# Some 390 unread matmuls behind the last useful one, with the moving operand in permuted pieces or the weights at a step

## The chip, the core and the metric

The kernel runs on one core of one Trainium2 chip. The metric is the device time of one execution in microseconds (us); lower is better. A core has five engines with queues of their own: TensorE (PE, with its weight loads shown apart as PEld), VectorE (DVE), ScalarE (ACT), GpSimd (POOL) and SyncE (SP, which here only issues DMAs). Results of PE land in PSUM, which has eight banks; everything that PE reads lies in SBUF, 128 partitions wide.

## The reference

Two stages follow each other. The first is an attention over 8 batches and 8 heads of width 64: 32 global rows attend to all 544 rows, and 512 local rows attend to the global ones and to a window of 32 to each side. The second is a two-layer MLP over all 4352 rows:

```python
x = np.ascontiguousarray(attn_out.transpose(0, 2, 1, 3)).reshape(B * S, H * D)   # 4352 x 512
h = x @ w_in                                                                     # 512 -> 2048
g = 0.5 * h * (1.0 + erf(h * inv_sqrt2))
return (g @ w_out).astype(np.float32)                                            # 2048 -> 512
```

All inputs and the output are float32.

## The kernel before, in words

**Precision.** Apart from the first stretch, which runs plain fp32 matmuls, every product is taken in a rounded 32-bit type (fp32r): an operand is split into a high part, which is the rounded value, and a low part, which is what is left. A product is then three matmuls: high by high, high by low and low by high.

**The MLP.** The rows are cut into 17 chunks of 256: two for each batch, and a last one with key "g" for all the global rows. For a chunk, `ml_hc` makes `h` for one of the 16 blocks of 128 hidden columns: four contraction steps of three matmuls each, whose weights (the stationary operand) are 128 columns of `wh` or `wl` and whose moving operand is 256 columns of `xh` or `xl` (L711 to L713). After the gelu and the split of its result, `ml_o` adds a block to the two output tiles `acc0` and `acc1`: weights are 128 columns of `gh` or `gl`, the moving operand is the 512 columns of `wh` or `wl` (L746 to L748). `ml_e` copies `acc` to `ob`, `ml_w` sends it out.

**The weights.** `w_4` (L175) lays the high parts of `w_in` and `w_out` into tiles of 1024 columns, two blocks of 512 in one tile (`wh`, 16 tiles of 4 KB in each partition). They stay there to the end.

**The order.** A planner written in the kernel sorts all steps by costs and due times and records them one after the other. It also ties every instruction to the one before it on its engine (`behind`), so that each queue stands in the planner's order. The attention of later batches is woven between the MLP of earlier ones; the last stretch of the program, from about 1000 us on, is the MLP of the chunk "g" alone. The last steps are the second half of its output: twelve matmuls into `acc1`, a copy of it on ACT, and DMAs from SP and ACT.

**PSUM.** The pool `ps_h` has two buffers of one bank each. `h` takes them in turn.

Of the kernel before, what the change touches and what calls it, by code (L numbers as in the profile page):

```python
# [8 lines left out]
F32 = mybir.dt.float32  # L9
# [75 lines left out]
def attn_mlp(ctx, tc, q_l, k_l, v_l, q_g, k_g, v_g, w_in, w_out, out):  # L85
    nc = tc.nc
    B, H, S, D = q_l.shape
# [3 lines left out]
    P = 128  # L91
    NCC = DM // P
    NF = FF // P
# [16 lines left out]
    ps_h = ctx.enter_context(tc.tile_pool(name="ps_h", bufs=2, space=PSUM))  # L110
# [7 lines left out]
    for half in range(2):  # L118
        m = (cp if half else mp).tile([P, WF], BF16, name=f"mask{half}")
# [10 lines left out]
    st = {}  # L130

    def copy(e, out, in_):
        if e == "a":
            nc.scalar.activation(out=out, in_=in_, func=AF.Copy)  # L134
        elif e == "v":
            nc.vector.tensor_copy(out=out, in_=in_)  # L136
        else:
            nc.gpsimd.tensor_copy(out=out, in_=in_)
# [5 lines left out]
    wp = ctx.enter_context(tc.tile_pool(name="wp", bufs=2 * NF + 1))  # L144
    wr = ctx.enter_context(tc.tile_pool(name="wr", bufs=NF))
    wraw, wf, wh, wl_ = {}, {}, {}, {}

    def w_load(e, n):
        f = n // 2
        wraw[n] = raw = wr.tile([P, 1024], I32, name="wraw", tag="wr")  # L150
        if n % 2 == 0:
            (nc.sync if e == "s" else nc.scalar).dma_start(
                out=raw.rearrange("p (c x) -> p c x", c=NCC),
                in_=w_in.bitcast(I32).rearrange("(c p) w -> p c w", p=P)[:, :, f * 256:(f + 1) * 256])
        else:
            (nc.sync if e == "s" else nc.scalar).dma_start(out=raw, in_=w_out.bitcast(I32)[f * P:(f + 1) * P, :])
# [18 lines left out]
    def w_4(e, i, n):  # L175
        if i % 2 == 0:
            wh["t"] = wr.tile([P, 1024], F32R, name="wh", tag="wr")
        wh[n] = wh["t"][:, i % 2 * 512:i % 2 * 512 + 512]
        copy(e, wh[n], wf[n])

# [606 lines left out]
    for i, n in enumerate(wl):  # L787
        due = 0.0
        step(("wl", n), w_load, (n,), WLE, due - 6.0, [("w1", wl[i - NW])] if i >= NW else [], [("wr", n)], issues=0.85, size=0.52, after=("wl", wl[i - 1]) if i else None)
        step(("w1", n), w_1, (n,), "av", due - 4.0, [("wl", n)])  # L790
        step(("w2", n), w_2, (n,), "a", due - 3.5, [("w1", n)])
        step(("w3", n), w_3, (n,), "v", due - 2.5, [("w2", n), ("w3", wl[i - 1]) if i else None], frees=[("wr", n)])
        used = [("mo", (0, 0), n // 2)] if n % 2 else [("hc", (0, 0), n // 2, c) for c in range(NCC)] if n // 2 < HQ or n // 2 == NF - 1 else [("h", (0, 0), n // 2)]
        step(("w4", n), w_4, (i, n), "va", due + 60.0, [("w3", wl[NF + i // 2]), ("wl", wl[-1])] + ([("w4", wl[i - 1])] if i else []), [("wr", ("h", n))] if i % 2 == 0 else [])
        step(("w5", n), w_5, (n,), "pv", due + 61.0, [("w4", n), ("w5", wl[i - 1]) if i else ("w3", wl[-1])] + used)

    for n, u in enumerate(units):
        b, half, p = u
        c = 2 * b + half
# [25 lines left out]
        else:  # L825
            last = [("tq", units[NPE - x]) for x in (3, 4)] if n < NPE + 2 else []
# [5 lines left out]
        w = n < NF32  # L832
# [19 lines left out]
        g = (b, p // 2) if half else None  # L852
# [59 lines left out]
    for n, key in enumerate(keys):  # L912
# [6 lines left out]
        for f in range(NF):  # L919
            hb = [("h", (key, f // 2))] if f % 2 == 0 else []  # L920
            w = [("w3", 2 * f)] if not n else [("w5", 2 * f)] if n == 1 else []
# [39 lines left out]
    while stack:  # L961
        x = stack.pop()
# [9 lines left out]
    for nm, x in nodes.items():  # L972
# [3 lines left out]
        else:  # L976
            c = 2 * nm[1][0] + nm[1][1] if len(nm) > 1 and isinstance(nm[1], tuple) else 99
# [7 lines left out]
    for x in nodes.values():  # L985
        y = x["after"]
# [21 lines left out]
    def starts(x, k):  # L1008
        t = x["at"][k]
        n = {}  # L1010
        for kind, y in x["takes"]:
            n[kind] = n.get(kind, 0) + 1
        for kind, m in n.items():
            h = sorted((freed.get(y, 1e9) for y in taken.get(kind, [])), reverse=True)
            i = bufs.get(kind, 1) - m
            if i < len(h):
                if h[i] == 1e9:
                    return None
                t = max(t, h[i] + LAT0)
        if k == "a" and x["size"]:  # L1020
            t = max(t, dma - 1.5)
        return t
# [4 lines left out]
    while any(ready.values()):  # L1027
        can = []
        for k in ENG:
            for x in ready[k]:  # L1030
                t = starts(x, k)
                if t is None:
                    continue
                t = max(t, busy[k])
                if k == "p" or k == "v" and x["port"]:
                    t = max(t, port)
# [11 lines left out]
        t, due, _, x, k = best  # L1048
# [33 lines left out]
    last, taker, w1s = {}, {}, {}  # L1082
# [5 lines left out]
    for t, i, x in order:  # L1088
        x["fn"](x["on"], *x["args"])
        ins = nc.cur_bb.bb.instructions  # L1090
# [12 lines left out]
            taker[kind] = ins[seen].name, ins[seen].engine  # L1103
        seen = len(ins)


# [1 line left out]
_INS = ['q_l', 'k_l', 'v_l', 'q_g', 'k_g', 'v_g', 'moe_w_in', 'moe_w_out']  # L1108
# [26 lines left out]
```

## Time and profile before

| | |
|---|---|
| time, median of 2 runs | 1045.17 us (1043.53 to 1046.81) |
| the profiled execution | 1045.66 us, of which 1043.8 us is the span from the first to the last instruction |
| granted TensorE clock, mean | 0.998 |
| PE busy | 1006.6 us, 96% of the span, 7000 matmuls |
| DVE, ACT, POOL busy | 66%, 65%, 36% |
| chain that ended last | PE 75%, ACT 7%, SP's queue 6%, DMA 5%, DVE 4% |

A matmul's listed duration holds its way through the array, which overlaps the next one; so the listed 0.28 us of a matmul with 256 columns isn't what it costs in a row of them. What it costs is the distance from one start to the next, and that is read from the timeline. A row of the timeline gives the start in us, the duration in us, the engine, the line, the operation, the tiles out<-in, and the shapes (contraction rows * output rows, then rows x columns of the moving operand).

### The profile page before, as it was taken

To read this page: it belongs to the slowest core of one execution; us is meant where nothing else is said; L and a number is where in the kernel's file an instruction comes from. 1 tells how busy PE (TensorE), PEld (TensorE's weight loads), DVE (VectorE), ACT (ScalarE), POOL (GpSimd) and SP (SyncE) were. 2 spreads that over 40 slices of the span, in tenths; PEclk is the share of its full clock that TensorE was granted. 3 is DMA by queue.
4 is the path that set the end of the run, shared out by engine and by line. 5 is a ranking of instruction groups with operands and counts; after the bars stand their busy time and mean duration, and the time that the engine had idled before them with its cause. 6 is when DMAs were issued, how large, how long until landed. Compare 5 with 4: busy or idle time off the path is not lost.

```text
span 1043.8 us, 21420 instructions
## 1 busy us (share of the span) xinstructions
PE 1006.6 (96%) x7000; PEld 894.8 (86%) x7000; DVE 684.9 (66%) x2089; ACT 677.0 (65%) x1617; POOL 379.7 (36%) x427
## 2 busy tenths in 40 slices
PE   3889999999998999999999999999999999999998
PEld 2666689989888989898999989998999989999997
DVE  2878978667676877777775777677776777572000
ACT  2868887667567866677675766677575766674232
POOL 2111576243332533343442524334343525233121
PEclk9999999999999999999999999999999999999999
DMA  6877232223221233223322232313322332101000
GB/s 165 239 207 260 51 72 54 49 45 77 57 59 36 38 77 66 63 39 60 79 43 55 55 82 53 65 31 61 82 39 57 62 71 58 48 14 56 1 21 21
DMA packets 277983, 72.29 MB, mean 69 GB/s; under 512 B 263152, under 2 KB 271344, under 8 KB 277872
## 3 DMA queue, kind: packets, MB, share of 16 engines
q1 hardware_dynamic: 271792, 68.57, 28.7%
q10 hardware_dynamic: 6080, 2.36, 0.9%
q8 instruction: 55, 0.90, 0.4%
q14 instruction: 56, 0.46, 0.1%
HBM read 61.41 MB, written 9.44 MB: 68 GB/s over the span
## 4 chain that ended last, share of the span: by engine, by line
PE 75%; ACT 7%; SPq 6%; DMA 5%; DVE 4%; issue 2%; POOL 1%; ACTq 0%; DVEq 0%; POOLq 0%
PE h L711 10%; PE acc L746 9%; PE h L712 9%; PE h L713 9%; PE acc L748 9%; PE acc L747 9%; PE o L519 5%; PE s L408 4%; PE acc L738 2%; PE t L482 2%; ACT a_t L281 2%; PE h L707 2%; PE go L652 2%; ACT L281 1%; DMA raws<-in_q_l_dram 1%
## 5 line engine op out<-in xcount | busy, mean ns | idle before, releaser
L141 POOL TENSOR_TENSOR gl<-gf,gh 128x512 fp32r<-128x512 f32 x127 | 167.8, 1321 | 400.4 <-ACT gh L134 280.1
L711 PE MATMUL h<-xh,wh 128*128 128x256 f32 x1024 | 296.6, 290 | 1.4 <-ACT gf L281 1.4
L712 PE MATMUL h<-xl,wh 128*128 128x256 f32 x1024 | 286.1, 279 | 0.0
L713 PE MATMUL h<-xh,wl 128*128 128x256 f32 x1024 | 285.6, 279 | 0.0
L746 PE MATMUL acc<-wh,gh 128*128 128x512 f32 x512 | 204.9, 400 | 0.0
L711 PEld LDWEIGHTS h<-xh,wh 128*128 128x128 f32 x1024 | 192.7, 188 | 10.2 <-ACT gf L281 1.8
L748 PE MATMUL acc<-wl,gh 128*128 128x512 f32 x512 | 200.4, 391 | 0.0
L747 PE MATMUL acc<-wh,gl 128*128 128x512 f32 x512 | 200.2, 391 | 0.0
L712 PEld LDWEIGHTS h<-xl,wh 128*128 128x128 f32 x1024 | 193.0, 188 | 5.7 <-issue 0.7
L713 PEld LDWEIGHTS h<-xh,wl 128*128 128x128 f32 x1024 | 193.9, 189 | 0.0
L281 ACT ACTIVATE gf<-h 128x512 f32<-128x512 f32 x136 | 81.2, 598 | 69.4 <-POOL gl L141 34.9
L281 ACT ACTIVATE a_t<-a_t,sm 128x192 f32<-128x192 f32 (+1 forms) x256 | 116.8, 458 | 1.9 <-DVE sm L433 1.1
L748 PEld LDWEIGHTS acc<-wl,gh 128*128 128x128 f32 x512 | 96.1, 188 | 21.1
L427 DVE CUSTOM_DVE_ANT_0 a_t<-s,mask 128x192 f32<-128x192 f32 (+1 forms) x256 | 80.4, 368 | 44.0 <-PE s L408 43.8
L134 ACT ACTIVATE gh<-gf 128x512 fp32r<-128x512 f32 x95 | 60.0, 632 | 75.7 <-PE acc L748 74.7
L746 PEld LDWEIGHTS acc<-wh,gh 128*128 128x128 f32 x512 | 96.3, 188 | 12.2
L747 PEld LDWEIGHTS acc<-wh,gl 128*128 128x128 f32 x512 | 96.4, 188 | 11.2
L134 ACT ACTIVATE at<-t 128x512 fp32r<-128x512 f32 (+1 forms) x112 | 59.5, 542 | 48.2 <-PE t L483 21.2
L502 DVE TENSOR_TENSOR at<-t,at 128x512 fp32r<-128x512 f32 (+1 forms) x112 | 67.5, 617 | 34.6 <-ACT at L134 33.9
L141 POOL TENSOR_TENSOR vs<-vr,vs 128x512 fp32r<-128x512 f32 x56 | 74.6, 1332 | 41.8 <-DVE vs L136 19.9
L281 ACT ACT_TABLE_LOAD x69 | 88.5, 1283 | 1.2
L550 DVE TENSOR_TENSOR xs<-o,xs 64x256 f32<-64x256 f32 x112 | 46.1, 412 | 49.0 <-ACT xs L545 47.9
(132 smaller groups left out, 1736.1 us busy)
## 6 DMA issues: line engine op xcount, KB each, us to landing
wraw<-in_moe_w_out_dram SPq DMA_DIRECT2D x16, 512.0 KB, 7.8
raws<-in_v_l_dram SPq DMA_DIRECT2D x64, 128.0 KB, 2.5
out_dram<-ob SPq DMA_DIRECT2D x32, 256.0 KB, 2.2
raws<-in_k_l_dram SPq DMA_DIRECT2D x224, 36.0 KB, 1.9
vr<-in_v_l_dram SPq DMA_DIRECT2D x113, 64.0 KB, 2.1
wraw<-in_moe_w_in_dram SPq DMA_DIRECT2D x14, 512.0 KB, 7.6
raws<-in_q_l_dram SPq DMA_DIRECT2D x224, 32.0 KB, 1.8
raws<-in_v_g_dram SPq DMA_DIRECT2D x128, 16.0 KB, 1.9
```

Of the source, the lines that this page charges most:

```text
L134: nc.scalar.activation(out=out, in_=in_, func=AF.Copy)
L141: (nc.vector if e == "v" else nc.gpsimd).tensor_sub(**kw)
L281: nc.scalar.activation(func=func, **kw)
L427: nc.vector.tensor_tensor_reduce(out=a_t[:, j, aoff[half][i]:aoff[half][i] + w], in0=s[:, c:c + w], in1=masks[half][i], scale=1.0, scalar= ...
L502: nc.vector.tensor_sub(out=at[:, 1], in0=st.pop((u, "t", j))[:, :n * P].rearrange("p (n q) -> p n q", q=P), in1=at.bitcast(F32)[:, 0])
L519: nc.tensor.matmul(out=o[:, :, qsl], lhsT=l.rearrange("p s e -> p (s e)"), rhs=r, start=(n == 0), stop=(n == 3), skip_group_check=True)
L711: nc.tensor.matmul(out=h, lhsT=hi, rhs=xh, start=(c == 0 and not (key == (0, 0) and f < HQ and f % 2)), stop=False, skip_group_check=True)
L712: nc.tensor.matmul(out=h, lhsT=hi, rhs=xl, start=False, stop=False, skip_group_check=True)
L713: nc.tensor.matmul(out=h, lhsT=lo, rhs=xh, start=False, stop=(c == NCC - 1), skip_group_check=True)
L746: nc.tensor.matmul(out=acc[t], lhsT=gh[:, f % 2, tsl], rhs=hi, start=(f == 0), stop=False)
L747: nc.tensor.matmul(out=acc[t], lhsT=gl[:, f % 2, tsl], rhs=hi, start=False, stop=False)
L748: nc.tensor.matmul(out=acc[t], lhsT=gh[:, f % 2, tsl], rhs=lo, start=False, stop=(f == NF - 1))
```

## The change

Every `wh` tile is remembered in a list `wr_t`. After the planner's steps have all been recorded, 390 more matmuls are recorded and tied to the end of PE's queue (`after_all`). Each reads high parts of weights, both as its stationary and as its moving operand, and writes into a bank of `ps_h` (tiles named `zaa`, `zab` and so on, in the two buffers by turns). Nothing reads these tiles. Each matmul starts its own sum (`start=True, stop=True`).

- `run(a, n, w, b, st_)` is a sequence of n equal matmuls into one bank: weights are 128 columns of the tile T5 that begin at column a, the moving operand is the first w columns of T1. With b over 1, `perm` puts the moving columns and the output columns into another order: the w columns are b parts, and pieces of 16 columns (64 bytes) are taken from the parts by turns. The output is permuted in the same way, so each product lands where it would have.
- With `st_` the weights are 128 columns at a step of 2, 4 or 8 columns.
- `mo` and `h` have the shape of an output step and a hidden step: two banks with three matmuls of 512 columns each, and one bank with twelve of 256, here with b = 2 and the weights moved by x columns. They are run by turns, eight times.

By columns of the moving operand that makes: 256 columns 270 times (6 plain, 80 with b = 2, 32 with b = 4, 40 with weights at a step of 2, 8 at a step of 4, 8 at a step of 8, 96 in the eight `h`), and 512 columns 120 times (48 with b = 2, 24 with weights at a step of 2, 48 in the eight `mo`). The 246 of the `run` calls are the matmuls "of no use" in the change's title; the 144 of `mo` and `h` are as unread.

```diff
     wraw, wf, wh, wl_ = {}, {}, {}, {}
+    wr_t = []
...
             wh["t"] = wr.tile([P, 1024], F32R, name="wh", tag="wr")
+            wr_t.append(wh["t"])
...
+    def after_all(e0):
+        ins = nc.cur_bb.bb.instructions
+        for y in ins[e0:]:
+            if y.engine in last:
+                behind(y, last[y.engine])
+            last[y.engine] = y.name
...
+    def bank(n):
+        return n, ps_h.tile([P, 512], F32, name="z" + next(code), tag="h")
+
+    def perm(x, b):
+        return x if b == 1 else x.rearrange("p (b a i) -> p a b i", b=b, i=16)
+
+    def mm(t, st_, mv, b=1):
+        nc.tensor.matmul(out=perm(t[:, 0:mv.shape[-1]], b), lhsT=st_, rhs=perm(mv, b), start=True, stop=True, skip_group_check=True)
...
+    T1, T2, T3, T5, T6, T7 = (wr_t[i] for i in (1, 3, 5, 7, 9, 11))
+
+    def run(a, n=8, w=256, b=1, st_=None):
+        _, t = bank(0)
+        for _ in range(n):
+            mm(t, T5[:, a:a + 128] if st_ is None else st_, T1[:, 0:w], b)
+
+    def mo(x, b):
+        t = [bank(0)[1] for _ in range(2)]
+        for i in range(2):
+            for m, g in ((T1, 0), (T1, 256), (T2, 0)):
+                mm(t[i], T5[:, 128 * i + g + x:128 * i + g + x + 128], m[:, 0:512], b)
+
+    def h(x, b):
+        _, t = bank(0)
+        for c in range(4):
+            for m, g in ((T3, T2), (T6, T2), (T3, T7)):
+                mm(t, g[:, c * 128 + x:c * 128 + 128 + x], m[:, 0:256], b)
+
+    run(0, 6)
+    for a in (0, 16, 32, 48, 8, 24, 40, 56):
+        run(a, 10, 256, 2)
+    for a in (0, 16, 32, 48, 8, 24, 40, 56):
+        run(a, 6, 512, 2)
+    for a in (0, 16, 32, 48):
+        run(a, 8, 256, 4)
+    for a in (0, 16, 32, 48):
+        run(0, 10, 256, 1, T5[:, a:a + 256:2])
+    for a in (0, 16, 32, 48):
+        run(0, 6, 512, 1, T5[:, a:a + 256:2])
+    run(0, 8, 256, 1, T5[:, 0:512:4])
+    run(0, 8, 256, 1, T5[:, 0:1024:8])
+    for x in (0, 16, 32, 48):
+        for _ in range(2):
+            mo(x, 2)
+            h(x, 2)
+    after_all(e0)
```

PE's queue before ends with the last output tile and the branch to the end of the program (`acc_13652` is `acc1` of the chunk "g"):

```order
L746 MATMUL acc_13652<-wh,gh 128x512
L747 MATMUL acc_13652<-wh,gl 128x512
L748 MATMUL acc_13652<-wl,gh 128x512
L746 MATMUL acc_13652<-wh,gh 128x512
L747 MATMUL acc_13652<-wh,gl 128x512
L748 MATMUL acc_13652<-wl,gh 128x512
L1130 UNCONDITIONAL_BRANCH
```

Now the same place, two lines further down in the file; a row is one instruction or several equal ones, and the bracket names the semaphore that it waits for (`PE_49` is the one that PE itself raises):

```order
L748 MATMUL acc_13652<-wh,gh 128x512
L749 MATMUL acc_13652<-wh,gl 128x512
L750 MATMUL acc_13652<-wl,gh 128x512
L1124 MATMUL zaa<-wh 128x256 [waits PE_49]
L1124 MATMUL zaa<-wh 128x256 x5
L1124 MATMUL zab<-wh 128x8x2x16 [waits PE_49]
L1124 MATMUL zab<-wh 128x8x2x16 x9
L1124 MATMUL zac<-wh 128x8x2x16 [waits PE_49]
L1124 MATMUL zac<-wh 128x8x2x16 x9
```

The new rows stand behind the last useful matmul, and the first matmul of each of the 55 new tiles waits for an earlier one of PE that used the same bank.

The middle of the new rows, on PE, where the permuted sequences with b = 4 give way to the weights at a step, and these to the eight turns of `mo` and `h`:

```order
L1124 MATMUL zaw<-wh 128x4x4x16 x8
L1124 MATMUL zax<-wh 128x256 x10
L1124 MATMUL zay<-wh 128x256 x10
L1124 MATMUL zaz<-wh 128x256 x10
L1124 MATMUL zba<-wh 128x256 x10
L1124 MATMUL zbb<-wh 128x512 x6
L1124 MATMUL zbc<-wh 128x512 x6
L1124 MATMUL zbd<-wh 128x512 x6
L1124 MATMUL zbe<-wh 128x512 x6
L1124 MATMUL zbf<-wh 128x256 x8
L1124 MATMUL zbg<-wh 128x256 x8
L1124 MATMUL zbh<-wh 128x16x2x16 x3
```

Nothing stands between them but more of PE's own rows; the queues of ACT, DVE, POOL and SP hold the same instructions in the same order as before.

More of the change, by code (lines that the diff above doesn't have):

```diff
@@ L1104, in attn_mlp @@
         seen = len(ins)
+    def after_all(e0):
[4 more added lines that the diff above has]
+            last[y.engine] = y.name
+    code = iter([a + b for a in "abcdefghijkmnpqrstuvwxyz" for b in "abcdefghijkmnpqrstuvwxyz"])
+    def bank(n):
[4 more added lines that the diff above has]
+        nc.tensor.matmul(out=perm(t[:, 0:mv.shape[-1]], b), lhsT=st_, rhs=perm(mv, b), start=True, stop=True, skip_group_check=True)
+    e0 = len(nc.cur_bb.bb.instructions)
+    H = [wh[n] for n in range(2 * NF)]
+    LO = [wl_[n] for n in range(2 * NF)]
+    key = "g"
+    X = [st["xh", key, c] for c in range(NCC)]
+    Y = [st["xl", key, c] for c in range(NCC)]
+    G = st[key, "gh", NF // 2 - 1].rearrange("p a b -> p (a b)")
+    T1, T2, T3, T5, T6, T7 = (wr_t[i] for i in (1, 3, 5, 7, 9, 11))
[31 more added lines that the diff above has]
+    after_all(e0)
 _INS = ['q_l', 'k_l', 'v_l', 'q_g', 'k_g', 'v_g', 'moe_w_in', 'moe_w_out']
```

## The prediction

> **What bounds the kernel now.** I read the page first: the busy line of PE, the granted clock and the chain that ended last.
>
> ```profile
> span 1043.8 us, 21420 instructions
> PE 1006.6 (96%) x7000; PEld 894.8 (86%) x7000; DVE 684.9 (66%) x2089; ACT 677.0 (65%) x1617; POOL 379.7 (36%) x427
> PEclk9999999999999999999999999999999999999999
> PE 75%; ACT 7%; SPq 6%; DMA 5%; DVE 4%; issue 2%; POOL 1%; ACTq 0%; DVEq 0%; POOLq 0%
> ```
>
> PE is busy for 96% of the span, holds 75% of the chain, and its clock is granted in full. The change touches only what comes behind PE's last useful matmul, so the next view is the timeline at the end of the span, and the busy time there in two windows (columns: length, then busy us and count of PE, PEld, DVE, ACT, POOL, then the granted clock, the DMA share and GB/s).
>
> ```profile
> 1039.10 0.39 PE L748 MATMUL acc<-wl,gh 128*128 128x512 f32 x1
> 1039.52 0.60 ACT L134 ACTIVATE ob<-acc 128x512 f32<-128x512 f32 x1 [0.76 <-PE acc L748]
> 1040.15 0.87 ACTq L761 DMA_DIRECT2D out_dram<-ob  x2
> 1038.79 2.73 SPq L761 DMA_DIRECT2D out_dram<-ob  x6
> ...
> 1030.00:1039.30 9.30, 9.30 (x48) 7.78 (x46) 0.69 (x1) 1.83 (x3) 0.67 (x1) 1.00 0.00 0
> 1039.30:1043.80 4.50, 0.19 (x1) 0.00 (x0) 0.00 (x0) 0.60 (x1) 0.00 (x0) 0.89 0.45 117
> ```
>
> PE has no gap up to its last matmul. After it come one copy of 0.60 us, the last output DMAs and the end of the program: 4.5 us in which PE is idle. That is all the cover there is for new work at the end of PE's queue.
>
> **What one more matmul costs.** Both shapes of the new matmuls stand in the last stretch, where PE alone works. I take the distance of starts over one hidden block and one output block; the rows between are left out.
>
> ```profile
> 1011.70 0.28 PE L711 MATMUL h<-xh,wh 128*128 128x256 f32 x1
> ...
> 1013.11 0.39 PE L746 MATMUL acc<-wh,gh 128*128 128x512 f32 x1
> ...
> 1014.47 0.28 PE L711 MATMUL h<-xh,wh 128*128 128x256 f32 x1
> ```
>
> Between the first two rows twelve matmuls of 256 columns start: (1013.11 − 1011.70) / 12 = 0.1175 us each. Between the last two stand six of 512 columns: 1.36 / 6 = 0.2267 us each. Each includes its weight load, which runs under the matmul before it. The new matmuls load weights once each too, so these are their prices if neither the order of pieces nor the step of the weights matters.
>
> The Trainium skill has a price for this: "TensorE: Matmul & The Clock Gate", section Back-to-back issue gap, gives N/2.4 + 2.5 ns for an isolated matmul at the full clock, which would be 109 and 216 ns here and a sum of 55.4 us instead of the one below. The trace is 8 to 11 ns above it per matmul, and the trace decides.
>
> **The change part by part.** The list of tiles costs nothing on the chip. The rest is 390 matmuls in PE's queue:
>
> - 270 of 256 columns: 270 × 0.1175 = 31.7 us
> - 120 of 512 columns: 120 × 0.2267 = 27.2 us
> - together 58.9 us.
>
> They could start at 1039.10 + 0.23 = 1039.33 and would be through at 1098.25; the last one, of 256 columns, ends 0.28 − 0.12 = 0.16 us later, at 1098.41. The copy on ACT and the output DMAs don't depend on them and go on as before, now hidden under PE. Then the end of the program follows. Its length I work out from the rows above: SP's six issues take 2.73 us, so the last one starts at about 1041.07. How long it takes to land is in the list of DMA issues (KB each, median us from issue to landing).
>
> ```profile
> out_dram<-ob SPq DMA_DIRECT2D x6, 64.0 KB, 1.8
> ```
>
> It lands at about 1042.9, and the span ends at 1043.8: 0.9 us for the barrier. So the new span is 1098.41 + 0.9 = 1099.3 us. The profiled execution took 1045.66 us for a span of 1043.8, which leaves 1.86 us outside; that makes 1101.2 us, 55.5 us more than before. The profiled run lies 0.5 us above the median of the runs shown, so I say 1101.
>
> **The waits.** The first matmul of each of the 55 tiles waits on PE's own semaphore. Such a wait stands in the program before too, at the second `h` tile of the chunk "g", behind the output step that ends here:
>
> ```profile
> 996.19 0.39 PE L748 MATMUL acc<-wl,gh 128*128 128x512 f32 x1
> 996.42 0.28 PE L711 MATMUL h<-xh,wh 128*128 128x256 f32 x1
> 996.54 0.28 PE L712 MATMUL h<-xl,wh 128*128 128x256 f32 x1
> ```
>
> The distances are 0.23 and 0.12 us, the same as without a wait. In the new code the matmul waited for is the last one of the bank two tiles earlier, and the tile between is at least three matmuls of 512 columns, 0.68 us, against the 0.39 us that one takes in all. Nobody else stands in PE's queue behind these waits that another engine needs. So 0 us; if that cover were gone, each would cost the rest of one matmul, 0.39 − 0.23 = 0.16 us, or 9 us for 55.
>
> **Permuted pieces.** 208 matmuls of 256 columns (16 pieces, 15 breaks) and 96 of 512 (32 pieces, 31 breaks) read and write in pieces of 16 columns. No row of before has such small pieces. The nearest has one break: `o` (L519) reads two pieces of 128 columns and writes two into PSUM.
>
> ```profile
> 627.82 0.64 PE L519 MATMUL o<-at,vs 128*128 128x256 f32 x4
> 628.29 0.42 PE L565 MATMUL sg<-k,gs 128*128 128x288 f32 x2
> ```
>
> Four of them take 628.29 − 627.82 = 0.47 us, 0.1175 each: the break costs nothing that 0.01 us over four matmuls can show. If each break cost 1 ns, the sum would be 208 × 15 + 96 × 31 ns = 6.1 us. At the other end stands half the pace, for which there are rows of the same sizes: the plain fp32 matmuls of the first chunk.
>
> ```profile
> 111.83 1.73 PE h L707 x8
> 113.56 1.72 PE acc L738 x4
> ```
>
> They start 0.216 and 0.43 us apart. At that pace the permuted ones cost 208 × 0.0985 + 96 × 0.203 = 40 us more. I take zero, since the nearest row shows zero; below zero is possible only by a little: the same `h` matmuls run slightly denser elsewhere.
>
> ```profile
> 599.74 0.28 PE L711 MATMUL h<-xh,wh 128*128 128x256 f32 x1
> ...
> 600.64 0.28 PE L713 MATMUL h<-xh,wl 128*128 128x256 f32 x1
> ```
>
> Eight in 0.90 us, 0.1125 each; for all 270 that is a gain of 1.4 us.
>
> **Weights at a step.** 56 matmuls of 256 columns and 24 of 512 load their 128 columns at a step of 8, 16 or 32 bytes. How much room a load has is seen where four follow each other with little else to do:
>
> ```profile
> 603.45 0.46 PEld L610 LDWEIGHTS gt<-ident,sgr 128*128 128x128 f32 x4
> 603.88 0.14 PEld L611 LDWEIGHTS gtg<-ident,sgr 128*128 128x128 f32 x1
> ```
>
> (603.88 − 603.45) / 4 = 0.1075 us for a load of consecutive columns. So a load has 0.01 us to spare under 256 columns and 0.12 us under 512. For a step, PE shows nothing; ACT does, reading every second 32-bit word (L167) against consecutive ones (L134):
>
> ```profile
> L167 ACT ACTIVATE wraw<-wraw 128x512 f32<-128x512 f32 x32 | 20.6, 669 | 0.0
> L134 ACT ACTIVATE ob<-acc 128x512 f32<-128x512 f32 x34 | 19.0, 597 | 10.7 <-PE acc L748 9.8 <-PE o L519 0.6
> ```
>
> That is 1.12 times, and 0.1075 × 1.12 = 0.120 us would add 0.2 us over the 56. I take that, as zero. The bound: twice the load, 0.215 us, costs 56 × 0.0975 = 5.5 us and stays hidden under 512 columns. If it grows with the step (2, 4, 8 times 0.1075), it is 40 × 0.0975 + 8 × 0.3125 + 8 × 0.7425 = 12.3 us.
>
> **The rivals.**
>
> - *Loads at a step are slow.* For it: only 0.01 us of room. Against it: ACT's row. 5.5 to 12.3 us more: 1107 to 1113.
> - *Pieces are slow.* PE breaks its stream at each piece, in SBUF or PSUM. For it: 16 or 32 pieces are far from the two of `o`. Against it: the break of `o` is free. Up to half the pace: 1141.
> - *The new matmuls aren't there.* Nothing reads the `z` tiles, and what turns the program into chip code may leave them out; the time would be 1045. It decides at the count of PE's matmuls, 7000 or 7390. For it: they have no reader. Against it: they stand in the program's order with waits that are kept. Any mixture that stays within 2% (20.9 us) would need the 390 to cost under 20.9 + 4.5 us, 65 ns each, and no row of 128 by 128 weights with 256 columns is under 112.
>
> The Trainium skill speaks for the first two: "SBUF — State Buffer", section SBUF: two separate sides, says that SBUF has lines of 16 bytes that want two hits each, PSUM lines of 8 bytes, and that any non-contiguous PSUM access slows matmuls significantly. Taken at its word that is the second rival; taken by its mechanism, pieces of 64 bytes fill their lines and cost nothing, while weights at a step of 4 or 8 columns hit each line once and pay. The row of `o` agrees with the mechanism more than with the word, though with one break only.
>
> **How the numbers follow.** Forecast, everything at the pace of the rows, with up to 1 ns per break: 72%, 1097 to 1107, likeliest 1101. Slow loads 14%; slow pieces 12%, mostly 1118 to 1141; not there 2%. The lower end takes twice the denser pace (2.7 us) and half the spread of the runs shown (1.6 us) off 1101; the upper end takes in the forecast and the slow loads, and a little of slow pieces: 1118. Outside remain most of slow pieces and the last rival. A measurement of this kernel tells about 2% from no change. Faster 1%, within 2% 2%, slower 97%.
>
> **What would show it.** PE has 7390 matmuls; DVE, ACT and POOL have their counts. The new rows start at 1039.3 without a gap and their starts are 0.117 and 0.227 us apart in every group; the end follows the last by about 1 us. If a group of weights at a step shows more, the first rival holds for it; if the groups with 8x2x16 columns do, the second. A gap at each new tile would show the waits wrong.

## The result and the profile after

The changed kernel takes 1099.99 us (median of 2 runs, 1099.91 to 1100.06) against 1045.17 us (median of 2 runs, 1043.53 to 1046.81). The ratio is 1.0524 with a 95% interval of 1.0453 to 1.0595: slower, by 54.8 us. The profiled execution took 1099.91 us for a span of 1098.1 us, so 1.8 us lie outside it, as before.

The page of the changed kernel, for the same lines as before:

```profile
PE 1069.9 (97%) x7390; PEld 952.6 (87%) x7390; DVE 681.8 (62%) x2089; ACT 676.9 (62%) x1617; POOL 380.2 (35%) x427
PE 82%; ACT 4%; SPq 3%; DVE 3%; DMA 2%; issue 1%; POOL 1%; DVEq 0%; ACTq 0%; POOLq 0%
```

PE has 390 matmuls more, and as many weight loads; DVE, ACT and POOL have the counts of before, and their busy times are within 3.1 us of before. The chain of waits ends in PE now, with the last new tile `zcg`, where before it went over to the copy `ob` on ACT.

The timeline of PE at the end of the changed kernel shows the last useful row and the first new ones, and after that the first tile of each group (start, time to the end of the row's last matmul, then the form and the count). The distance from one tile's start to the next, over the count, is the pace.

```profile
1034.09 0.39 PE L750 MATMUL acc<-wl,gh 128*128 128x512 f32 x1
1034.32 0.88 PE L1124 MATMUL zaa<-wh 128*128 128x256 f32 x6
1035.03 1.36 PE L1124 MATMUL zab<-wh 128*128 128x256 f32 x10
...
1044.66 1.60 PE L1124 MATMUL zaj<-wh 128*128 128x512 f32 x6
...
1056.18 1.10 PE L1124 MATMUL zat<-wh 128*128 128x256 f32 x8
...
1059.97 1.36 PE L1124 MATMUL zax<-wh 128*128 128x256 f32 x10
...
1064.77 1.57 PE L1124 MATMUL zbb<-wh 128*128 128x512 f32 x6
...
1070.35 1.92 PE L1124 MATMUL zbf<-wh 128*128 128x256 f32 x8
1072.11 2.10 PE L1124 MATMUL zbg<-wh 128*128 128x256 f32 x8
1074.04 0.88 PE L1124 MATMUL zbh<-wh 128*128 128x512 f32 x3
...
1095.64 1.60 PE L1124 MATMUL zcg<-wh 128*128 128x256 f32 x12
```

The first new matmul starts 0.23 us behind the last useful one, and no row has an idle time in front of it. The last tile is through at 1095.64 + 12 × 0.12 = 1097.08, and the span ends 1.0 us later. So the 390 took 1097.08 − 1034.32 = 62.76 us, where the sum of the prediction had 58.93 us. By group, in us (in this table b = 2 and b = 4 stand for the permuted groups, and "summed" is the prediction's price times the count):

| group | matmuls | summed | took | more | ns each |
|---|---|---|---|---|---|
| `zaa`, 256 consecutive | 6 | 0.71 | 0.71 | 0.00 | 118 |
| 256, b = 2 (`zab` on) | 80 | 9.40 | 9.63 | 0.23 | 120.4 |
| 512, b = 2 (`zaj` on) | 48 | 10.88 | 11.52 | 0.64 | 240.0 |
| 256, b = 4 (`zat` on) | 32 | 3.76 | 3.79 | 0.03 | 118.4 |
| 256, weights at step 2 (`zax` on) | 40 | 4.70 | 4.80 | 0.10 | 120.0 |
| 512, weights at step 2 (`zbb` on) | 24 | 5.44 | 5.58 | 0.14 | 232.5 |
| 256, weights at step 4 (`zbf`) | 8 | 0.94 | 1.76 | 0.82 | 220 |
| 256, weights at step 8 (`zbg`) | 8 | 0.94 | 1.93 | 0.99 | 241 |
| eight turns of `mo` and `h`, b = 2 (`zbh` on) | 48 + 96 | 22.16 | 23.04 | 0.88 | 240.0 and 120.0 |

Within `zbf` the second matmul starts 121 ns after the first and the others 233 to 235 ns after one another; that is why its mean is 220.

The tail answers to the forecast. The block is 3.8 us longer than forecast; yet the total is 1.0 us under the forecast. That is because the part that both kernels share ended earlier in this execution: the last useful matmul starts at 1034.09, before at 1039.10. The first 100 us in the view by windows, of the kernel before and then of the changed one (the window, its length, then busy us and count of PE, PEld, DVE, ACT and POOL, granted clock, DMA share, GB/s):

```profile
0.00:100.00 100.00, 75.50 (x404) 54.54 (x405) 64.97 (x193) 65.19 (x159) 16.71 (x39) 0.98 0.78 227
```

```profile
0.00:100.00 100.00, 79.62 (x419) 57.47 (x420) 67.39 (x198) 66.99 (x164) 16.92 (x39) 1.00 0.78 228
```

By then PE has started 419 matmuls instead of 404, although the queues hold the same instructions up to there. The granted clock differs too, 0.98 against 1.00. The change doesn't reach this part, so the first experiment asks whether the early end is chance.

### The profile page after: what moved, and what is told of

Read it like the earlier page. It is cut to its first block, busy times and chain, and to the rows that moved or that the text cites. A ratio compares the mean times of both kernels' runs of the same rounds, so it can differ in the third digit from the quotient of the medians.

```text
span 1098.1 us, 22201 instructions
## 1 busy us (share of the span) xinstructions
PE 1069.9 (97%) x7390; PEld 952.6 (87%) x7390; DVE 681.8 (62%) x2089; ACT 676.9 (62%) x1617; POOL 380.2 (35%) x427
## 4 chain that ended last, share of the span: by engine, by line
PE 82%; ACT 4%; SPq 3%; DVE 3%; DMA 2%; issue 1%; POOL 1%; DVEq 0%; ACTq 0%; POOLq 0%
PE h L713 10%; PE h L714 10%; PE h L715 10%; PE acc L748 9%; PE acc L750 9%; PE acc L749 9%; PE o L521 5%; PE s L410 4%; PE t L484 2%; PE acc L740 2%; PE go L654 2%; PE h L709 2%; PE sg L567 1%; PE t L485 1%; ACT L283 1%
```

## The experiments

All of them change only what stands behind the last useful matmul, except the last two, which have no such block at all. Nothing reads the results of the block in any of them.

### The same kernel again

No edit.

> The changed kernel once more. In its profile the last useful matmul started at 1034.09 us, 5.0 us earlier than in the profile of the kernel before (1039.10), and the 390 new ones took 62.8 us from start to start instead of the forecast 58.9. Theory A (the two executions differ by chance in the part that both share): on the same chip the changed kernel costs 62.8 + 1.0 - 4.5 = 59 us more than the one before, give or take the 3 us that runs of the kernel before spread. Theory B (the longer program makes the shared part faster): it costs 54 to 55 us more again, and the last useful matmul starts near 1034 again.

Measured: 1101.81 us (4 runs, 1101.24 to 1104.75) against 1043.06 us on the same chip, a ratio of 1.0565 (1.0542 to 1.0588), or 58.75 us more. The timeline of PE:

```profile
1036.51 0.39 PE L750 MATMUL acc<-wl,gh 128*128 128x512 f32 x1
1036.74 0.88 PE L1124 MATMUL zaa<-wh 128*128 128x256 f32 x6
...
1098.07 1.60 PE L1124 MATMUL zcg<-wh 128*128 128x256 f32 x12
```

The block again takes 1098.07 + 1.44 − 1036.74 = 62.77 us. By the trace the change should cost 62.76 + 1.02 − 4.5 = 59.3 us on an equal shared part, and this chip shows 58.75. So Theory A held and Theory B fell: the 5.0 us that the shared part seemed to gain are not of the change. In the nine profiles of this study that have the same instructions up to there, the last useful matmul started between 1034.09 and 1039.48, and the two of the comparison happened to lie near opposite ends of that. The interval of the first comparison, 1.0453 to 1.0595, holds the 1.0565 of this one.

A part of this chance has a cause that the profiles show. In the kernel before there is a stretch of 3.4 us with half the clock granted (the last three numbers of the row are the granted clock, the DMA share and GB/s):

```profile
66.60:70.00 3.40, 3.40 (x12) 2.41 (x9) 3.13 (x14) 3.37 (x6) 0.34 (x2) 0.50 1.08 299
```

The changed kernel's first profile has no such stretch, and its shared part ended earliest, at 1034.09. The five profiles with one stretch before the last useful matmul had it at 1035.84 to 1039.10, the three with two of them, or one twice as long, at 1037.43 to 1039.48. At half the clock 3.4 us hold the work of 1.7, so one stretch can explain up to 1.7 us of the 5.0 (an estimate). Where the rest comes from was not found.

### Nothing permuted, nothing at a step

```
-        run(a, 10, 256, 2)
+        run(a, 10, 256)
...
-        run(0, 10, 256, 1, T5[:, a:a + 256:2])
+        run(0, 10, 256, 1, T5[:, a:a + 128])
...
-    run(0, 8, 256, 1, T5[:, 0:512:4])
+    run(0, 8, 256, 1, T5[:, 0:128])
...
-            mo(x, 2)
-            h(x, 2)
+            mo(x, 1)
+            h(x, 1)
```

and so for every other line of the block: the same 390 matmuls, all consecutive.

> The same 390 matmuls, with consecutive moving columns and consecutive weights throughout. Theory A (pieces and steps carry the surcharge): 0.1175 and 0.2267 us each, 58.9 us in all, so 3.9 us less than the changed kernel on the same chip. Rival (the surcharge comes from the operands that are used, repeated weights and one moving tile): no difference, 62.8 us. Shared part earlier or not as for the run before.

Measured: 1099.8 us (4 runs, 1097.63 to 1100.15), a ratio of 1.0535 (1.0515 to 1.0556); 2.0 us less than the changed kernel by the medians, whose intervals overlap, so the traces have to decide. In the timeline of PE the block takes 1097.01 − 1037.26 = 59.75 us (its last tile, 1095.60 + 12 × 0.1175, ends at 1097.01):

```profile
1037.26 0.88 PE L1124 MATMUL zaa<-wh 128*128 128x256 f32 x6
...
1047.45 1.55 PE L1124 MATMUL zaj<-wh 128*128 128x512 f32 x6
...
1058.62 1.11 PE L1124 MATMUL zat<-wh 128*128 128x256 f32 x8
...
1062.40 1.36 PE L1124 MATMUL zax<-wh 128*128 128x256 f32 x10
...
1074.62 0.86 PE L1124 MATMUL zbh<-wh 128*128 128x512 f32 x3
...
1081.66 1.53 PE L1124 MATMUL zbr<-wh 128*128 128x256 f32 x12
1083.02 0.85 PE L1124 MATMUL zbs<-wh 128*128 128x512 f32 x3
...
1095.60 1.58 PE L1124 MATMUL zcg<-wh 128*128 128x256 f32 x12
```

Pieces and steps together cost 62.76 − 59.75 = 3.0 us. Stretch by stretch, the changed kernel against this one: `zaa` to `zax`, where the first pieces stand, 25.65 − 25.14 = 0.5 us; `zax` to `zbh`, the weights at a step, 14.07 − 12.22 = 1.85 us; from `zbh` on, the eight turns in pieces, 23.04 − 22.39 = 0.65 us. So the pieces cost 1.2 us and the steps 1.85. The other 0.8 us that the sum lacked have nothing to do with either: consecutive matmuls don't have one pace. The 48 of 512 columns from `zaj` to `zat` take 11.17 us, 232.7 ns each and not 226.7, and the twelve of `zbr` 113.3 ns each and not 117.5. Neither expectation had that: theory A put the whole 3.9 us on pieces and steps, the rival nothing.

### The block twice

```
+    for _t in range(2):
+        run(0, 6)
...
```

with the rest of the block in the loop too: 780 matmuls.

> The block of 390 matmuls two times, 780 in all. Theory A (the cost is additive, PE has no slack): 62.8 us more than the changed kernel, whatever the shared part does. Rival (a part of the cost is paid once: the first weights, the code of the new stretch, the clock): less than 62.8 for the second block, the groups of the first slower than those of the second.

Measured: 1166.64 us (4 runs, 1165.94 to 1168.07), a ratio of 1.1178 (1.1155 to 1.1202); 64.8 us more than with one block. The timeline of PE, at the first tile of the second block and the last tile:

```profile
1102.48 0.87 PE L1124 MATMUL zch<-wh 128*128 128x256 f32 x6
```

```profile
1163.80 1.60 PE L1124 MATMUL zep<-wh 128*128 128x256 f32 x12
```

The second block takes 1163.80 + 1.44 − 1102.48 = 62.76 us, the same as the first (1102.48 − 1039.71 = 62.77). The two profiled executions differ by 1168.07 − 1102.35 = 65.7 us, 3.0 more than a block, and the shared part is 1039.48 − 1036.51 = 3.0 us longer in this one; the 2 us of the medians fit that. So the block's price adds up, nothing of it is paid only once, and it has no cover but the 4.5 us of the tail.

### Which side of a matmul dislikes pieces

The block is replaced by groups of six matmuls of 512 and ten of 256 columns with the same weights and the same 512 columns of the moving operand. The moving operand, the output or both are cut in pieces of 64, 32, 16, 8 or 4 columns (`go(n, w, i, 1, 0)` cuts the moving operand alone, `go(n, w, i, 0, 1)` the output alone).

```
+    for n, w in ((6, 512), (10, 256)):
+        go(n, w)
+        for i in (64, 32, 16, 8, 4):
+            go(n, w, i)
+        for i in (32, 16, 8, 4):
+            go(n, w, i, 1, 0)
+        for i in (32, 16, 8, 4):
+            go(n, w, i, 0, 1)
+        go(n, w)
```

> In place of the 390: groups of 6 matmuls with 512 columns and of 10 with 256, same weights, in this order for each size: consecutive; moving and output both in pieces of 64, 32, 16, 8, 4 columns; only the moving operand in pieces of 32, 16, 8, 4; only the output in pieces of 32, 16, 8, 4; consecutive. In the changed kernel pieces of 16 took 0.240 us for 512 columns and 0.120 for 256, which is 7.5 ns a piece in both. Theory H1 (each break adds 13.3 ns / 31 = 0.43 ns to the consecutive pace): 512 columns take 0.254 in pieces of 8 and 0.281 in pieces of 4. Theory H2 (a piece of 16 takes the time of 18 columns, 240/576 = 0.417 ns each, and the consecutive pace is a floor): pieces of 64 and 32 cost nothing over 0.2267, pieces of 8 take 0.267, pieces of 4 take 0.320; for 256 columns 0.1175, 0.1175, 0.120, 0.133, 0.160. If the output (PSUM) is the cause, groups with only the moving operand cut run at the consecutive pace; if the reads are, those with only the output cut do.

Measured (one run, 1078.31 us), the timeline of PE at 512 columns: `zaa` is consecutive and `zab` has both cut in pieces of 64; `zaf` has both in pieces of 4, `zag` the moving operand alone in pieces of 32 and `zah` in pieces of 16; `zam` and `zan` have the output alone in pieces of 16 and 8:

```profile
1036.07 1.52 PE L1161 MATMUL zaa<-wh 128*128 128x512 f32 x6
1037.43 1.52 PE L1161 MATMUL zab<-wh 128*128 128x512 f32 x6
...
1043.10 1.69 PE L1161 MATMUL zaf<-wh 128*128 128x512 f32 x6
1044.62 1.59 PE L1161 MATMUL zag<-wh 128*128 128x512 f32 x6
1046.05 1.60 PE L1161 MATMUL zah<-wh 128*128 128x512 f32 x6
1047.49 1.62 PE L1161 MATMUL zai<-wh 128*128 128x512 f32 x6
...
1051.86 1.52 PE L1161 MATMUL zam<-wh 128*128 128x512 f32 x6
1053.22 1.52 PE L1161 MATMUL zan<-wh 128*128 128x512 f32 x6
```

The distances over six are, in ns a matmul of 512 columns (consecutive 227, at the start and the end of the series):

| pieces of | 64 | 32 | 16 | 8 | 4 |
|---|---|---|---|---|---|
| both | 227 | 235 | 240 | 243 | 253 |
| moving operand alone | | 238 | 240 | 243 | 253 |
| output alone | | 232 | 227 | 227 | 227 |

The runs with both and with the moving operand alone agree, and the output alone in pieces of 16, 8 or 4 runs at the consecutive pace. So it is the read of the moving operand that pays; the write into PSUM in pieces of 16, 8 or 4 is free, and the 232 ns at pieces of 32 lie inside the 227 to 235 that consecutive matmuls show elsewhere in this study. The 13.3 ns are counted from the densest consecutive pace; from the 232.7 ns of the plain block's 48 it is 7. The cost doesn't go by the break: pieces of 16 cost 13.3 ns more for 31 breaks, pieces of 4 cost 27 ns for 127 breaks. Both theories had far more: 254 and 267 ns at pieces of 8, 281 and 320 at pieces of 4. At 256 columns the same cuts give 120 ns for 16, 123 for 8 and 128 for 4, against 119 consecutive.

The Trainium skill, "SBUF — State Buffer", section SBUF: two separate sides (its box on "cachelines"), says that any non-contiguous PSUM access slows matmuls significantly. Here the output in pieces of 4 columns, 16 bytes, runs at the consecutive 226.7 ns, so for pieces of that size and more the measurement differs and decides.

### How the price of a load grows with the step

```
+    for n, w in ((8, 512), (12, 256)):
+        for s in (1, 2, 3, 4, 5, 6, 8, 1):
+            go(n, w, T5[:, 0:128 * s:s])
```

`go(n, w, st_)` makes n matmuls of w columns with the weights `st_`; `s` is the step. Nothing is permuted here; only the weights' step changes.

> In place of the 390: consecutive moving columns, weights of 128 columns at steps of 1, 2, 3, 4, 5, 6, 8 and 1 again; 8 matmuls of 512 columns in each group, then 12 of 256. In the changed kernel 256 columns took 0.120 us at step 2, 0.233 at step 4 and 0.242 at step 8; 512 columns 0.232 at step 2. Theory: a load is slow once its 32-bit elements lie 16 bytes or more apart, and then it is slow by about two whatever the step. So for 256 columns 0.118 to 0.120 at steps 1 to 3, and 0.23 to 0.24 at 4, 5, 6 and 8; for 512 columns nothing above 0.245. Rival: the load slows with every further byte of the step; then step 3 lies near 0.17, and 5 and 6 between 4 and 8.

Measured (one run, 1072.45 us), the timeline of PE at 256 columns, from step 1 to step 8 and step 1 again:

```profile
1052.08 1.59 PE L1159 MATMUL zai<-wh 128*128 128x256 f32 x12
1053.50 1.60 PE L1159 MATMUL zaj<-wh 128*128 128x256 f32 x12
1054.94 2.24 PE L1159 MATMUL zak<-wh 128*128 128x256 f32 x12
1057.02 2.96 PE L1159 MATMUL zam<-wh 128*128 128x256 f32 x12
1059.82 2.90 PE L1159 MATMUL zan<-wh 128*128 128x256 f32 x12
...
1065.30 3.06 PE L1159 MATMUL zaq<-wh 128*128 128x256 f32 x12
1068.19 1.59 PE L1159 MATMUL zar<-wh 128*128 128x256 f32 x12
```

In ns each: 118 at step 1, 120 at step 2, 173 at step 3, 233 at step 4, 228 at steps 5 and 6, 241 at step 8. It rises between 2 and 4 and is nearly flat from there. So the theory missed step 3, and the rival missed 5 and 6. That it is the load that grows is seen in the loads themselves, which the profile lists (PEld, by form; busy us, then mean ns of one): 189 and 195 ns at steps 1 and 2, 260 at 3, 329 at 4, 322 at 5 and 6, 338 at 8. The row of step 4:

```profile
L1159 PEld LDWEIGHTS zam<-wh 128*128 128x128 f32 x12 | 2.9, 329 | 0.0
```

Under 512 columns, where a matmul has room, steps 2 to 6 take 234 to 238 and step 8 takes 243, against 226 and 232 for step 1 at the two ends of the series: a load of up to 0.24 us stays under such a matmul but for a few ns.

A count that fits steps 3 to 6: at step s the 128 words lie in 32 s groups of four words, and in 128 groups from step 4 on. 173 / 96 = 1.80 ns a group at step 3, 228 to 233 / 128 = 1.78 to 1.82 from step 4 to 6. At step 2 it would give 64 × 1.8 = 115 ns, which a stream of 120 ns covers. At step 1 it would give 58 ns, and the prediction's row of loads with little else to do had 107.5; so below step 3 something else sets the load's length. Step 8 lies 5% above the count, and nothing here says why.

The Trainium skill, "SBUF — State Buffer", the same section and box, states that SBUF has lines of 16 bytes, which is four of these words, and that each line wants two hits. By it, step 4 and more pay one line for each word, and the plateau agrees. The box gives no price; here it is 1.8 ns a line from step 3 to 6.

### Does the load disturb the stream?

```
+    for n, w in ((8, 512), (12, 256)):
+        for i in (0, 16, 4):
+            for c in (128, 96, 64, 32):
+                go(n, w, T5[:, 0:c], i, c)
```

The weights have c = 128, 96, 64 or 32 columns, and so has the output its partitions; i is the size of the pieces, 0 for consecutive. With fewer columns the load that runs beside the stream is shorter: the profile lists a mean of 189 ns for the loads of `zae` with 128 columns and of 111 for those of `zah` with 32.

> In place of the 390: weights of 128, 96, 64 and 32 columns, each with consecutive moving columns, with pieces of 16 and with pieces of 4; 8 matmuls of 512 columns in each group, then 12 of 256. With 128 weight columns the first three take 0.2267, 0.240 and 0.250 us for 512. Theory (the load of the next weights reads beside the stream of the moving operand, and the two get in each other's way): what lies over about 0.215 shrinks with the load, to a half at 64 columns and a quarter at 32: 0.218, 0.221 and 0.224 at 32 columns. Rival (the stream itself is slow in pieces, load or no load): the three stay at 0.2267, 0.240 and 0.250 whatever the weights' columns.

Measured (one run, 1080.86 us), the timeline of PE, pieces of 16 at 512 columns (`zae` to `zah`), then 256 consecutive columns with 32 columns of weights (`zar`):

```profile
1045.01 2.08 PE L1159 MATMUL zae<-wh 128*128 128x512 f32 x8
...
1050.77 2.08 PE L1159 MATMUL zah<-wh 128*32 128x512 f32 x8
1052.68 2.17 PE L1159 MATMUL zai<-wh 128*128 128x512 f32 x8
...
1064.82 1.52 PE L1159 MATMUL zar<-wh 128*32 128x256 f32 x12
1066.18 1.60 PE L1159 MATMUL zas<-wh 128*128 128x256 f32 x12
```

Pieces of 16 take 239 to 241 ns at every size of the weights, and pieces of 4 take 251, 248, 246 and 248 from 128 down to 32 columns. So they are not slow because a load gets in their way, as the rival had it; the stream itself is slower, 240 / 512 = 0.469 ns a column against 226.7 / 512 = 0.443. For consecutive columns the load may matter where it has least room: 256 columns take 120, 116, 114 and 113 ns from 128 down to 32 columns of weights. But some steps of the plain block reach the same 113.3 ns with 128 columns of weights, so one group of each size doesn't settle it. 113.3 / 256 is 0.443 ns a column too, about the densest stream seen in these groups. At 512 consecutive columns a smaller load gains nothing: 226, 231, 229 and 233 ns from 128 down to 32.

### What sets the consecutive pace: place or history?

```
+    for b in (1, 2):
+        for xo in (0, 16, 32, 48):
+            for xh_ in ((0, 16, 32, 48) if b == 1 else (xo,)):
+                for _ in range(3):
+                    mo2(xo, 1)
+                    h(xh_, b)
```

An output step with its weights at column offset `xo`, then a hidden step with its weights at `xh_`, each pair three times.

> In place of the 390: output step (6 matmuls of 512 columns) and hidden step (12 of 256) by turns, consecutive columns, three times for each of the 16 pairs of weight offsets 0, 16, 32 and 48 columns; then four offsets with the hidden step in pieces of 16. In the plain kernel the hidden step took 0.120 us a matmul at offset 0, 0.113 at 16 and 0.118 to 0.119 at 32 and 48. Theory (the offset between weights and moving operand sets the pace): the hidden step takes 0.113 at offset 16 whatever came before. Rival (it is set by what came before): the same offset takes different paces after different output steps. The pair takes 2.77 us in the kernel before, and 12 x 0.1133 + 6 x 0.2267 = 2.72 at best.

Measured (one run, 1209.64 us), the timeline of PE. `zam` is the hidden step at offset 16 after an output step at 0, `zbz` the one at 16 after an output step at 16; `zbi` and `zbm` are the second and third of the same pair, offset 48 after 0:

```profile
1048.10 1.58 PE L1124 MATMUL zam<-wh 128*128 128x256 f32 x12
1049.51 0.86 PE L1124 MATMUL zan<-wh 128*128 128x512 f32 x3
...
1067.80 1.58 PE L1124 MATMUL zbi<-wh 128*128 128x256 f32 x12
1069.22 0.88 PE L1124 MATMUL zbj<-wh 128*128 128x512 f32 x3
...
1070.62 1.52 PE L1124 MATMUL zbm<-wh 128*128 128x256 f32 x12
1071.98 0.85 PE L1124 MATMUL zbn<-wh 128*128 128x512 f32 x3
...
1081.84 1.53 PE L1124 MATMUL zbz<-wh 128*128 128x256 f32 x12
1083.20 0.85 PE L1124 MATMUL zca<-wh 128*128 128x512 f32 x3
```

The same hidden step takes 117.5 ns a matmul in `zam` and 113.3 in `zbz`, and even two repeats of one pair take 118.3 and 113.3. Over all pairs the hidden step takes 113 to 121 ns and the output step 227 to 234. The place sorts most of it: at offset 16 all nine hidden steps after output steps at 16, 32 and 48 take 113 to 114 ns, and only the three after an output step at 0 take 118; at offsets 0 and 32 all 24 take 118 to 121. So place and what ran before both matter, and since repeats of one pair differ, the two together don't fix the pace either. Pieces of 16 take 120 ns at every offset.

### Moving the useful operands by 64 bytes

If place matters, it can be had or lost in the useful part, and a better place would be a gain. Two versions of the kernel before, without any block, open their pools of SBUF in another order and change nothing else. The first moves `xh`, `xl` and the rounded weights by 64 bytes modulo 256, the second `xh` and `xl` without the weights; in both, small tiles of the attention (a mask, or the pool `sg`) move along:

```
-    mp = ctx.enter_context(tc.tile_pool(name="mp", bufs=1))
...
+    wp = ctx.enter_context(tc.tile_pool(name="wp", bufs=2 * NF + 1))
+    wr = ctx.enter_context(tc.tile_pool(name="wr", bufs=NF))
+    mp = ctx.enter_context(tc.tile_pool(name="mp", bufs=1))
...
-    wp = ctx.enter_context(tc.tile_pool(name="wp", bufs=2 * NF + 1))
-    wr = ctx.enter_context(tc.tile_pool(name="wr", bufs=NF))
```

> The kernel before, without new matmuls; its SBUF pools are opened in another order, which moves xh and xl and the weight tiles by 64 bytes: in bytes from a multiple of 256, the moving operand of h starts at 192 instead of 128 and its weights at 0 instead of 192, as in the hidden steps at offset 16 of the run before, which took 0.113 to 0.114 us a matmul; the moving operand of acc starts at 0 instead of 192. Theory (the place of the operands sets the pace): the 3072 matmuls of h go from a mean of 0.116 to 0.114 us, 6 to 8 us less in all, unless acc (1536 matmuls at a mean of 0.229) loses it: between 1036 and 1044 us. Rival (what runs before sets it): h stays at 0.116 and the time at that of the kernel before.

```
-    xp = ctx.enter_context(tc.tile_pool(name="xp", bufs=1))
     sg = ctx.enter_context(tc.tile_pool(name="sg", bufs=2))
+    xp = ctx.enter_context(tc.tile_pool(name="xp", bufs=1))
```

> The kernel before with two pools swapped: xh and xl move by 64 bytes, the weights stay, so that both start 192 bytes past a multiple of 256, as in the hidden steps at offset 0 of the run before, which took 0.119 to 0.120 us. acc is untouched. Theory (place): h at 0.119, 8 to 10 us more than the kernel before. Rival (history): no difference.

Measured: the first 1046.91 us (10 runs, 1045.19 to 1049.53), a ratio of 1.0039 (1.0028 to 1.0051); the second 1053.47 us (4 runs, 1051.05 to 1054.08), a ratio of 1.0088 (1.0065 to 1.0112), both against 1042.9 us for the kernel before on the same chip. Neither is faster. The mean listed duration of `h` in L712 goes from 279 ns to 280 and to 283.

In the distances of starts, over all that follow each other within a tile without a gap, the mean of `h` is 116.3 ns before, 116.5 with both moved and 119.2 with `xh` and `xl` moved; that of `acc` is 229.0, 231.7 and 231.5. With `xh` and `xl` moved, 3072 × 2.9 ns + 1536 × 2.5 ns = 12.7 us are to be expected and 10.6 us are there; with both, 3072 × 0.2 ns + 1536 × 2.7 ns = 4.8 us against 4.0. So 64 bytes of place are worth 1% of this kernel. In the second version the theory of place holds for `h`, whose 119 ns it had forecast. But nothing that `acc` reads was moved there (`gh`, `gl`, `wh` and `wl` keep their places), and it became slower all the same; that it pays for what ran before it is likely, and not shown. In the first version `h` didn't gain the 2 ns that the place of offset 16 promised, and the rival, which had the time unchanged, missed the 4 us that `acc` lost. Of the three layouts the one of the kernel before is the fastest, and of all versions run here it stays the fastest.

## Why the prediction was right, and where its sum was not

**390 matmuls in PE's queue, not removed, 4.5 us of cover.** Right. PE has 7390 matmuls, the new ones start 0.23 us behind the last useful one, and the block run twice costs 62.76 us each time. The span ends 1.0 us after the last one is through by the pace, where the forecast had 0.16 + 0.9.

**The price of one.** 0.1175 and 0.2267 us were read from one quiet stretch and taken for all. With nothing permuted the block takes 59.75 us against 58.93, so this term was 0.8 us too small: from tile to tile the pace wanders between 113 and 121 ns and between 227 and 235 ns, with place and history. The denser pace that was weighed as a gain of 1.4 us shows in two of the eight hidden steps of the plain block, and nowhere in the changed kernel.

**The waits at no cost.** Right: no idle time at any of the 55 tiles.

**Pieces at no cost.** This is one of two terms put at nothing that cost something. The table has 1.8 us for it (0.23 + 0.64 + 0.03 + 0.88), but 0.6 of that is the price of consecutive matmuls, which was too low; against the plain block the pieces cost 1.2 us. It stayed under the bound of 1 ns a break, which had 6.1 us: the most that 512 columns pay is 13.3 / 31 = 0.43 ns. The row of `o` couldn't show it, since it has two pieces of 128 columns, and pieces of 64 are still free. The rival of half the pace fell. It named SBUF or PSUM, and the experiment with the sides apart shows that it is the read from SBUF alone.

**Weights at a step at no cost.** Nearly right for step 2, where ACT's row pointed: 0.24 us for 64 matmuls by the table, 0.1 against the plain block. Wrong for steps 4 and 8: these 16 matmuls took 220 and 241 ns, 1.8 us in all. ACT's row had no step above 2, and the row beside it copies `acc`, so it set a read of SBUF against one of PSUM. There the bound "twice the load" was the right one, and the one that grows with the step was not: from step 4 to 8 the matmul grew from 233 to 241 ns. The rival held for 16 matmuls and not for the 56 that it was priced for; the 40 at step 2 take 120 ns. So it was worth 1.8 us and not 5.5 to 12.3.

**The spread.** Half the spread of the runs shown, 1.6 us, was put in for the part that both kernels share. The profiles show it ending anywhere in 5.4 us. In the comparison it gave back 5.0 us by chance, up to 1.7 of them by a stretch at half the clock, which hid the 3.8 us that the sum lacked. Beside runs of the kernel before on one chip the change costs 58.75 us, 3.3 us more than the forecast of 55.5; on top of 1045.17 that is 1103.9, still inside the forecast's own 1097 to 1107. The direction and the mechanism were right for the reason given; that the number was within 1.0 us was luck.

## What to carry to other kernels

Work behind the last useful instruction of the engine that bounds the kernel costs its full length less the idle tail, and that can be summed from the distance of starts in the nearest quiet stretch; expect the sum to be off by a per cent or two (59.75 against 58.93 us here), because that distance depends on how operands lie. For matmuls like these (128 columns of 32-bit weights), a moving operand cut in pieces of 64 bytes costs 3 to 6% of a matmul of 512 columns, by the consecutive pace it is compared with; an output in pieces of 16 bytes or more costs nothing; and weights at a step of four words or more double a matmul of 256 columns and add at most 16 ns to one of 512. Before a profile's end is compared with another's, see how far the same instructions scatter, here 5 us of 1040, and whether the clock was granted in full in both.

## What the runs showed of the hardware that was not expected

- With weights at a step, a matmul of 256 columns takes 120 ns at step 2, against 118 consecutive, 173 ns at step 3 and 228 to 241 ns from step 4 to 8. That is a plateau, not a slope.
- The price of pieces lies in the read of the moving operand and is the same with weights of 128 or 32 columns (239 to 241 ns at pieces of 16). It grows slowly, from 235 ns at pieces of 32 columns to 253 at pieces of 4, where there are eight times as many breaks.
- Moving `xh` and `xl` by 64 bytes makes the whole kernel 1.0088 times as long. Why that place is worse was not tried further, and stays open; so does why a tile's pace depends on the tile before it.
- Eight of nine profiles have a stretch of 3.4 us at a granted clock of 0.50 before the last useful matmul, or two, or one twice as long; the one without ended its shared part earliest, at 1034.09 us.
